# Linformer attention and a feed-forward layer on one core: k and v projections placed next to a burst of quarter-array matmuls, and v's last heads projected ahead of the third tile of values in the opening

## Chip, cores, metric

One core of one Trainium2 chip. The metric is the device time of one execution in microseconds.

## The reference, cut to what matters

```python
# q, k, v: (8 batches, 8 heads, 1024, 64); E, F: (64, 1024)
k_proj = np.einsum('ks,bhsd->bhkd', E, k)
v_proj = np.einsum('ks,bhsd->bhkd', F, v)
scores = q @ k_proj^T / sqrt(64)
attn   = exp(scores - max) / (sum(...) + 1e-9)
x      = (attn @ v_proj), heads side by side      # (8192, 512)
h      = x @ w_in                                  # (8192, 2048)
out    = (h * sigmoid(1.702 h)) @ w_out            # (8192, 512)
```

The last two lines are nearly all of the arithmetic. The kernel cuts the 8192 tokens into 16 blocks of 512; two blocks make a batch.

## The kernel before

The kernel writes its own order of instructions. Blocks are a first layer (16 groups of 4 full-array matmuls, slots 0 to 15) and a second (8 half-tiles of 8 full-array matmuls, slots `O` to `O + 7`). Attention work for later blocks is put between them by `at(block, slot, ...)`. TensorE's results land in PSUM; this kernel writes a bank of it anew only after another engine has read the results out, and it takes the banks of each pool in turn.

```python
def proj(b):                     # k and v of one batch: 128*64 tiles, two side by side
    def go():
        kvps[b] = f_tile([P, H, D])
        for j in range(J):
            for e, r in enumerate((LO, HI)):
                nc.tensor.matmul(kvps[b][r], eft[:, j, e * KP:(e + 1) * KP],
                                 (kt, vt)[e][b][:, :, j, :],
                                 start=(j == 0), stop=(j == J - 1))
    return go

def four(outs, lhsTs, rhss):     # 64*64 tiles, four at once: scores, denominators, numerators
    for i, ro in ((0, (LO, HI)), (1, (HI, LO))):
        for ri, r in zip((LO, HI), ro):
            nc.tensor.matmul(outs[i][r], lhsTs[i][ri], rhss[i][ri], start=True, stop=True)

# ... (cut) the opening
v_out(0, proj0(1, 0, 4), 0, 2)
for u in range(2):
    scores(0, u, 0)()
v_out(0, proj0(1, 4, 2), 2, 1)
for p in range(3):
    tok(0, p, 0)()
v_out(0, proj0(1, 6, 2), 3, 1, nc.scalar.copy)
for p in range(3):
    x_tr(0, p, 0)()
tok(0, 3, 0)()
q_tr(0, 1)()
x_tr(0, 3, 0)()

# ... (cut) where the projections and the bursts go
for b in range(2, B):
    j = max(2, NB2 * b - 3)
    at(j, 2, proj(b))
    at(j, 3, kv_out(b))          # DVE copies k and v out of the projection's PSUM bank
    if b > 2:
        at(NB2 * b - 4, O, q_dma(b))
for j in range(3, NBLK - 2):
    for u in range(2):
        if j + 3 < NBLK:
            at(j, O + 5 * u, scores(j + 3, u))
        at(j, O + 5 * u, norm(j + 2, u))
    if j + 3 < NBLK:
        at(j, O + 6, gelu_table)
```

The softmax here doesn't subtract the row's maximum and nothing guards it: scores larger than these inputs give would overflow.

Of the kernel before, what the change touches and what calls it, by code (L numbers as in the profile page):

```python
# [17 lines left out]
def kernel(ctx, tc, q, k, v, E, F,  # L18
                                                     moe_w_in, moe_w_out, out):
    nc = tc.nc  # L20
    B, H, S, D = q.shape
# [4 lines left out]
    NB2 = S // 512  # L26
# [90 lines left out]
    def f_tile(shape, dt=F32):  # L117
        return ps_f.tile(shape, dt, name="f_ps")
# [20 lines left out]
    def proj(b):  # L139
# [9 lines that stand above are left out]
    def proj0(e, h0, n):  # L149
        ps = f_tile([P, n, D])  # L150
        for j in range(J):
            nc.tensor.matmul(ps, eft[:, j, :], (kt, vt)[e][0][:, h0:h0 + n, j, :],
                             start=(j == 0), stop=(j == J - 1))
        return ps
# [14 lines left out]
    def v_out(b, v_ps, p0, n, cp=nc.vector.tensor_copy):  # L169
        if b < 2:  # L170
            if n == 1:
                for r, t in ((LO, p0 % 2), (HI, 1 - p0 % 2)):
                    cp(vxs[b][r, 2 * p0 + t, :D], v_ps[HI, t, :])
            else:
                vv = v_ps[HI].rearrange("k (u x) d -> k u x d", x=4)
                vx = vxs[b][:, 2 * p0:2 * (p0 + n), :D].rearrange("k (u x) d -> k u x d", x=4)
                for r, xs_ in ((LO, X_LO), (HI, X_HI)):
                    cp(vx[r, :, xs_], vv[:, :, xs_])
        if b > 0:
            vv = v_ps[HI].rearrange("k (u x) d -> k u x d", x=4)  # L180
            for r, xs_ in ((LO, X_LO), (HI, X_HI)):
                nc.vector.tensor_copy(vqs[b % 2][r].rearrange("k (u e) d -> k u e d", e=2), vv[:, :, xs_, :])

    def kv_out(b):
        def go():
            ps = kvps.pop(b)
            k_b = att.tile([KP, H, D], BF16, name="k_b")
            nc.vector.tensor_copy(k_b, ps[LO])
            if b > 1:
                nc.sync.dma_start_transpose(out=kts[b % 2], in_=k_b.rearrange("k h d -> k (h d)"))  # L190
            v_out(b, ps, 0, HP)
            kbs[b] = k_b
        return go

    def q_tr(b, g):
        def go():
            if g == 0:
                qT[b] = att.tile([P, J, HP, P], BF16, name="qT")
            t_ps = f_tile([P, 2, HP, P], BF16)
            for jj in range(2):  # L200
                j = 2 * g + jj
                if b == 0:
                    for h in range(H):
                        r = h % 2 * D
                        nc.tensor.transpose(t_ps[r:r + D, jj, h // 2, :], qt[0][:, h, j, :], ident)  # L205
                else:
                    for p in range(HP):
                        nc.tensor.transpose(  # L208
                            t_ps[:, jj, p, :],
                            qt[b][:, j, 2 * p:2 * p + 2, :].rearrange("s t d -> s (t d)"), ident)  # L210
            nc.vector.tensor_copy(qT[b][:, 2 * g:2 * g + 2], t_ps)  # L211
        return go

    def q_dma(b):
        def go():
            qT[b] = att.tile([P, J, HP, P], BF16, name="qT")
            nc.sync.dma_start_transpose(out=qT[b].rearrange("r j p s -> r (j p) s"),
                                        in_=qt[b].rearrange("s j h d -> s (j h d)"))
        return go

    def four(outs, lhsTs, rhss):
# [5 lines that stand above are left out]
    def scores(h, u, half=None):  # L227
        b, c = divmod(h, NB2)
        j0, n = (c * JB, JB) if half is None else (c * JB + half * JB // 2, JB // 2)
        ts = slice(j0 * P - c * TB, (j0 + n) * P - c * TB)  # L230

        def go():
            if h not in expT:
                expT[h] = att.tile([P, HP, TB], BF16, name="expT", bufs=3)
            s_ps = [f_tile([P, n * P]) for _ in range(2)]
            four(s_ps, [kts[b % 2][:, 2 * u + i, :] for i in range(2)],
                 [qT[b][:, j0:j0 + n, 2 * u + i, :] for i in range(2)])
            for i in range(2):
                nc.scalar.activation(expT[h][:, 2 * u + i, ts], s_ps[i], AF.Exp, scale=scale)  # L239
        return go  # L240
# [4 lines left out]
    def x_of(h):  # L245
        if h not in xT:
            xT[h] = att.tile([P, KC, TB], BF16, name="xT", bufs=3)
        return xT[h]

    def norm(h, u):  # L250
        def go():
            e = [expT[h][:, 2 * u + i, :] for i in range(2)]
            d_ps = [ps_d.tile([P, TB], F32, name="d_ps") for _ in range(2)]
            four(d_ps, [ones, ones], e)
            n_ps = [ps_n.tile([P, TB], F32, name="n_ps") for _ in range(2)]
            four(n_ps, [vqs[h // NB2 % 2][:, 2 * u + i, :] for i in range(2)], e)
            for i in range(2):
                rden = att.tile([P, TB], F32, name="rden")
                nc.vector.reciprocal(rden, d_ps[i])  # L259
                nc.vector.tensor_tensor(x_of(h)[:, 2 * u + i, :], n_ps[i], rden, op=ALU.mult)  # L260
        return go
# [5 lines left out]
    def tok(h, p, half):  # L267
        def go():
            d_ps = f_tile([P, 4, D + 1]) if (h, half) == (0, 0) and p > 1 else                 ps_d.tile([P, 4, D + 1], F32, name="d_ps")
            for i in range(2):  # L270
                t = 2 * half + i
                nc.tensor.matmul(d_ps[:, 2 * i:2 * i + 2, :].rearrange("s t d -> s (t d)"),  # L272
                                 expT[h][:, p, t * P:(t + 1) * P],
                                 vxs[h // NB2][:, 2 * p:2 * p + 2].rearrange("r t d -> r (t d)"),
                                 start=True, stop=True)
            rd = work.tile([P, 4, 1], F32, name="rd")
            nc.vector.reciprocal(rd, d_ps[:, :, D:])  # L277
            xs[h, p, half] = work.tile([P, 4, D], BF16, name="x_sb", bufs=4)
            nc.vector.tensor_tensor(xs[h, p, half], d_ps[:, :, :D], rd.to_broadcast([P, 4, D]), op=ALU.mult)
        return go  # L280

    def x_tr(h, p, half):
        def go():
            x_sb = xs.pop((h, p, half)).rearrange("s (i t) d -> s i (t d)", i=2)
            n_ps = ps_n.tile([P, 2, P], BF16, name="n_ps")
            for i in range(2):
                nc.tensor.transpose(n_ps[:, i, :], x_sb[:, i, :], ident)  # L287
            cp = nc.scalar.copy if (h, half) == (0, 0) else nc.vector.tensor_copy
            cp(x_of(h)[:, p, half * TB // 2:(half + 1) * TB // 2], n_ps.rearrange("r i s -> r (i s)"))
        return go  # L290
# [53 lines left out]
    def at(j, slot, *fs):  # L344
        fill.setdefault((j, slot), []).extend(fs)

    O = FC
# [6 lines left out]
    v_out(0, proj0(1, 0, 4), 0, 2)  # L354
    for u in range(2):
        scores(0, u, 0)()
    v_out(0, proj0(1, 4, 2), 2, 1)
    for p in range(3):
        tok(0, p, 0)()
    v_out(0, proj0(1, 6, 2), 3, 1, nc.scalar.copy)  # L360
    for p in range(3):
        x_tr(0, p, 0)()
    tok(0, 3, 0)()
    q_tr(0, 1)()
    x_tr(0, 3, 0)()

# [27 lines left out]
        at(1, O + 3 + p, x_tr(2, p, 0), x_tr(2, p, 1))  # L394
    at(2, 1, norm(3, 0))
    at(2, 11, norm(3, 1))
    for b in range(2, B):
        j = max(2, NB2 * b - 3)
        at(j, 2, proj(b))
        at(j, 3, kv_out(b))  # L400
        if b > 2:
            at(NB2 * b - 4, O, q_dma(b))
    for j in (1, 2):
        at(j, O + 5, gelu_table)
    at(2, O + 5, norm(4, 0))
    at(3, 4, norm(4, 1))
    for j in range(3, NBLK - 2):
        for u in range(2):
            if j + 3 < NBLK:
                at(j, O + 5 * u, scores(j + 3, u))  # L410
            at(j, O + 5 * u, norm(j + 2, u))
        if j + 3 < NBLK:
            at(j, O + 6, gelu_table)

    def filled(j, slot):
        for f in fill.pop((j, slot), []):
# [45 lines left out]
```

## Time and profile before

| | before |
|---|---|
| time, median of the first 3 runs | 518.31 us (518.21 to 518.4) |
| TensorE busy | 98% of the span, clock 1.0 |
| VectorE (DVE), ScalarE (ACT) busy | 49%, 51% |
| one steady batch (two blocks) | 60.71 us |

A timeline line gives the start and length in us, the engine, the source line, the output and input, the array tile of a matmul (128*128 full, 128*64 half, 64*64 quarter), the operand's shape and the count. A bracket says how long the engine had been idle and what released it. Ends of matmuls are modelled, so all arithmetic uses starts. The lines for before stand in the prediction.

### The profile page before, as it was taken

Reading aid. Unit: us, or ns where it says so; the run is one execution under the profiler, and the core shown is the slowest. Engines: PE = TensorE matmul, PEld = TensorE weight load, DVE = VectorE, ACT = ScalarE, POOL = GpSimd, SP = SyncE. Lnnn points to the kernel's source line nnn. Section 1 sums busy time; section 2 is a strip of 40 time slices with the busy share of each in tenths; the row PEclk is TensorE's granted clock in tenths of the full one; section 3 lists DMA queues with packets and bytes.
Section 4 is the critical chain, followed back from the end, with each engine's and each line's share of the span. In section 5 each row is a group of like instructions: output and inputs, shape, how many; then the busy total and the mean of one; then the engine's idle time right before and its main releaser. Section 6 shows DMA issues by size and latency. Waiting matters only on the chain.

```text
span 516.5 us, 6729 instructions
## 1 busy us (share of the span) xinstructions
PE 506.9 (98%) x2856; PEld 233.2 (45%) x2856; DVE 251.4 (49%) x231; ACT 264.0 (51%) x439; POOL 77.4 (15%) x96
## 2 busy tenths in 40 slices
PE   6899999999999999999999999999999999999997
PEld 3584454444444444444444444444444444444444
DVE  3533324766774672818547282655818275560000
ACT  1575464555646456474555645465473646344351
POOL 6442620821510024000510000000000000000000
PEclk9999999999999999999999999999999999999999
DMA  9999999999996039550694201060200101010102
GB/s 162 197 203 207 217 180 182 165 191 159 241 152 162 1 90 166 106 133 0 147 176 121 53 41 48 0 164 0 84 4 1 81 1 81 1 82 1 81 1 82
DMA packets 113950, 53.78 MB, mean 104 GB/s; under 512 B 87680, under 2 KB 111488, under 8 KB 112000
## 3 DMA queue, kind: packets, MB, share of 16 engines
q0 software_dynamic: 84384, 29.37, 50.2%
q1 hardware_dynamic: 29456, 23.73, 16.6%
q8 instruction: 22, 0.36, 0.3%
q10 hardware_dynamic: 80, 0.26, 0.1%
q14 instruction: 8, 0.07, 0.0%
HBM read 59.24 MB, written 16.78 MB: 147 GB/s over the span
## 4 chain that ended last, share of the span: by engine, by line
PE 94%; DMA 4%; POOL 1%; issue 0%; DVE 0%; DVEq 0%; POOLq 0%
PE f_ps L333 43%; PE f_ps L301 42%; PE f_ps L144 3%; DMA w_in_sb<-in_moe_w_in_dram 2%; DMA v_sb<-in_v_dram 2%; PE f_ps L225 2%; PE d_ps L225 1%; PE n_ps L225 1%; PE f_ps L325 1%; PE n_ps L287 0%; PE d_ps L272 0%; PE f_ps L208 0%; POOL k_sb L57 0%; PE f_ps L205 0%; POOL q_sb L57 0%
## 5 line engine op out<-in xcount | busy, mean ns | idle before, releaser
L259 DVE RECIPROCAL rden<-d_ps 128x512 f32<-128x512 f32 x52 | 174.4, 3353 | 149.0 <-PE d_ps L225 149.0
L301 PE MATMUL f_ps<-xT,w_in_sb 128*128 128x512 bf16 (+1 forms) x1088 | 228.4, 367 | 0.2
L333 PE MATMUL f_ps<-w_out_sb,gT 128*128 128x512 bf16 x1008 | 227.0, 379 | 0.0
L304 ACT ACTIVATE gT<-f_ps 128x512 bf16<-128x512 f32 (+1 forms) x268 | 153.7, 575 | 85.4 <-PE f_ps L301 84.4
L301 PEld LDWEIGHTS <-w_in_sb 128*128 128x128 bf16 x1088 | 104.5, 98 | 116.4 <-issue 4.3
L333 PEld LDWEIGHTS <-gT 128*128 128x128 bf16 x1008 | 95.7, 98 | 120.4 <-issue 11.1
L336 ACT COPY o_sb<-f_ps 128x512 f32<-128x512 f32 x63 | 37.0, 587 | 133.5 <-PE f_ps L333 123.7
L63 POOL DMA_DIRECT2D q_sb<-in_q_dram x56 | 49.1, 894 | 67.5 <-DMA k_sb<-in_k_dram 27.7
L239 ACT ACTIVATE expT<-f_ps 128x512 bf16<-128x512 f32 (+1 forms) x68 | 35.2, 574 | 14.4 <-PE f_ps L225 14.4
L260 DVE TENSOR_TENSOR xT<-n_ps,rden 128x512 bf16<-128x512 f32 x52 | 36.0, 692 | 5.4
L327 DVE COPY o_sb<-f_ps 128x256 f32<-128x256 f32 x1 | 0.4, 424 | 50.9 <-PE f_ps L325 50.9
L57 POOL DMA_DIRECT2D k_sb<-in_k_dram x9 | 7.8, 864 | 103.7 <-PE f_ps L144 101.4
L239 ACT ACT_TABLE_LOAD x13 | 16.7, 1283 | 4.7 <-PE f_ps L225 4.5
L243 ACT ACT_TABLE_LOAD x14 | 18.0, 1283 | 0.3
L225 PE MATMUL f_ps<-qT,kt 64*64 64x512 bf16 (+1 forms) x136 | 13.8, 386 | 0.4 <-ACT expT L239 0.4
L144 PE MATMUL f_ps<-k_sb,eft 128*64 128x512 bf16 x56 | 13.4, 382 | 0.0
L144 PE MATMUL f_ps<-v_sb,eft 128*64 128x512 bf16 x56 | 13.4, 382 | 0.0
L211 DVE COPY qT<-f_ps 128x1024 bf16<-128x1024 bf16 x8 | 5.5, 692 | 12.4 <-PE f_ps L205 6.8
L277 DVE RECIPROCAL rd<-d_ps 128x4 f32<-128x4 f32 x22 | 3.8, 175 | 15.5 <-PE d_ps L272 15.4
L225 PEld LDWEIGHTS <-kt 64*64 64x64 bf16 x136 | 4.0, 103 | 14.3 <-issue 14.3
L225 PE MATMUL d_ps<-expT,ones 64*64 64x512 bf16 x104 | 10.2, 381 | 0.0
L225 PE MATMUL n_ps<-expT,vq 64*64 64x512 bf16 x104 | 10.0, 376 | 0.0
(57 smaller groups left out, 127.0 us busy)
## 6 DMA issues: line engine op xcount, KB each, us to landing
out_dram<-o_sb SPq DMA_DIRECT2D x15, 1024.0 KB, 4.5
k_sb<-in_k_dram POOLq DMA_DIRECT2D x7, 1024.0 KB, 13.5
v_sb<-in_v_dram POOLq DMA_DIRECT2D x7, 1024.0 KB, 10.7
q_sb<-in_q_dram POOLq DMA_DIRECT2D x56, 128.0 KB, 11.1
w_in_sb<-in_moe_w_in_dram POOLq DMA_DIRECT2D x8, 256.0 KB, 12.7
w_out_sb<-in_moe_w_out_dram POOLq DMA_DIRECT2D x4, 512.0 KB, 14.7
k_sb<-in_k_dram POOLq DMA_DIRECT2D x2, 512.0 KB, 8.0
out_dram<-o_sb SPq DMA_DIRECT2D x3, 256.0 KB, 2.0
```

The costliest lines, as they stand in the source:

```text
L57: nc.gpsimd.dma_start(out=dst[b][:, h:h + n, js:js + jn], in_=sv[:, h:h + n, js:js + jn])
L63: nc.gpsimd.dma_start(out=qt[b][:, j], in_=qv[:, j])
L144: nc.tensor.matmul(kvps[b][r], eft[:, j, e * KP:(e + 1) * KP], (kt, vt)[e][b][:, :, j, :], start=(j == 0), stop=(j == J - 1))
L225: nc.tensor.matmul(outs[i][r], lhsTs[i][ri], rhss[i][ri], start=True, stop=True)
L239: nc.scalar.activation(expT[h][:, 2 * u + i, ts], s_ps[i], AF.Exp, scale=scale)
L243: nc.scalar.preload_act_table(AF.Gelu_apprx_sigmoid)
L259: nc.vector.reciprocal(rden, d_ps[i])
L260: nc.vector.tensor_tensor(x_of(h)[:, 2 * u + i, :], n_ps[i], rden, op=ALU.mult)
L301: nc.tensor.matmul(h_ps, w_in_sb[:, kc, fc * P:(fc + 1) * P], xT[j][:, kc, ts], start=(kc == 0), stop=(kc == KC - 1))
L304: nc.scalar.activation(gts[j][:, fc, ts], h_ps, AF.Gelu_apprx_sigmoid)
L333: nc.tensor.matmul(o_ps[n], gts[j][:, fc, n * P:(n + 1) * P], w_out_sb[:, fc, :], start=(fc == 0), stop=(fc == FC - 1))
L336: nc.scalar.copy(osb[j][:, n, :], o_ps.pop(n))
```

## The change

TensorE pays something each time the shape of its tiles changes (0.09 to 0.12 us in the trace of before, worked out in the prediction). The change puts the projections of batches 4 to 7 directly ahead of a burst of quarter tiles, so that one return to full tiles falls away. In the opening it is meant to fill waits for DVE with other work.

```diff
     for u in range(2):
         scores(0, u, 0)()
+    for p in range(2):
+        tok(0, p, 0)()
     v_out(0, proj0(1, 4, 2), 2, 1)
-    for p in range(3):
-        tok(0, p, 0)()
+    x_tr(0, 0, 0)()
     v_out(0, proj0(1, 6, 2), 3, 1, nc.scalar.copy)
-    for p in range(3):
-        x_tr(0, p, 0)()
+    tok(0, 2, 0)()
+    x_tr(0, 1, 0)()
     tok(0, 3, 0)()
+    x_tr(0, 2, 0)()
     q_tr(0, 1)()
     x_tr(0, 3, 0)()
 ...
-    for b in range(2, B):
-        j = max(2, NB2 * b - 3)
-        at(j, 2, proj(b))
-        at(j, 3, kv_out(b))
-        if b > 2:
-            at(NB2 * b - 4, O, q_dma(b))
 ...
+    at(2, 2, proj(2))
+    at(2, 3, kv_out(2))
+    for b in range(3, B):
+        j = NB2 * b - 4
+        at(j, O, q_dma(b))
+        at(j, O + 6, proj(b), kv_out(b))
 ...
             if j + 3 < NBLK:
-                at(j, O + 5 * u, scores(j + 3, u))
-            at(j, O + 5 * u, norm(j + 2, u))
+                at(j, O + 6 * u, scores(j + 3, u))
+            at(j, O + 6 * u, norm(j + 2, u))
         if j + 3 < NBLK:
-            at(j, O + 6, gelu_table)
+            at(j, O + 7, gelu_table)
```

## The prediction

> **What bounds the kernel now.** I read the page's busy line and chain first, then TensorE's timeline over one pair of steady blocks, then its weight loads, then the opening.
>
> ```profile
> PE 506.9 (98%) x2856; PEld 233.2 (45%) x2856; DVE 251.4 (49%) x231; ACT 264.0 (51%) x439; POOL 77.4 (15%) x96
> ...
> PEclk9999999999999999999999999999999999999999
> ...
> PE 94%; DMA 4%; POOL 1%; issue 0%; DVE 0%; DVEq 0%; POOLq 0%
> ```
>
> TensorE is busy 98% of the span at full clock and carries 94% of the chain; every other engine is about half idle. So only two things can move the time: what TensorE itself spends between its matmuls, and the few places where it waits. The timeline of blocks 3 and 4 (two blocks make one batch) shows the first kind (start, duration, engine, line):
>
> ```profile
> 170.07 1.89 PE L333 MATMUL f_ps<-w_out_sb,gT 128*128 128x512 bf16 x8
> 171.89 0.41 PE L225 MATMUL f_ps<-qT,kt 64*64 64x512 bf16 x4
> 172.13 0.39 PE L225 MATMUL d_ps<-expT,ones 64*64 64x512 bf16 x4
> 172.34 0.39 PE L225 MATMUL n_ps<-expT,vq 64*64 64x512 bf16 x4
> 172.66 8.81 PE L333 MATMUL f_ps<-w_out_sb,gT 128*128 128x512 bf16 x40
> ...
> 185.64 2.75 PE L301 MATMUL f_ps<-xT,w_in_sb 128*128 128x512 bf16 x12
> 188.32 0.40 PE L144 MATMUL f_ps<-k_sb,eft 128*64 128x512 bf16 x1
> ...
> 190.17 11.40 PE L301 MATMUL f_ps<-xT,w_in_sb 128*128 128x512 bf16 x52
> 201.40 1.89 PE L333 MATMUL f_ps<-w_out_sb,gT 128*128 128x512 bf16 x8
> ```
>
> Work with starts only, since the ends are modelled. The 64 matmuls of an undisturbed first layer (156.25 to 170.07) take 13.82 us, 0.216 us each. A burst of 12 quarter tiles (64*64, four at once) should cost 3 x 0.216 = 0.65 us, but the gap from 171.89 to 172.66 is 0.77, and the burst began 0.09 late (170.07 + 8 x 0.216 = 171.80). So it costs about 0.09 to enter and 0.12 to leave. Scores, denominators and numerators inside it follow each other with 0.24, 0.21: no further toll between bursts of one shape. The k and v projection (128*64, two at once) should take 8 x 0.216 = 1.73: it starts 0.09 after 185.64 + 12 x 0.216 = 188.23, and from 188.32 to 190.17 is 1.85, again 0.12 to leave. **One detour costs 0.21 to 0.22 us**, in either shape. The same sum for whole layers agrees: 201.40 - 185.64 = 15.76, less 13.82, less 1.73, is 0.21.
>
> The weight loads show why:
>
> ```profile
> 185.42 2.47 PEld L301 LDWEIGHTS <-w_in_sb 128*128 128x128 bf16 x12
> 188.32 1.44 PEld L144 LDWEIGHTS <-eft 128*64 128x64 bf16 x16 [0.42 <-issue]
> 190.16 1.84 PEld L301 LDWEIGHTS <-w_in_sb 128*128 128x128 bf16 x10 [0.41 <-issue]
> ```
>
> Between equal shapes a load starts 0.22 us ahead of its matmul (185.42 against 185.64) and is hidden; where the shape changes it starts with the matmul (188.32, 190.16), after some 0.4 us without a load. A load takes 98 to 109 ns by the groups, about the size of the toll.
>
> **What the Trainium skill says.** "TensorE: Matmul & The Clock Gate", section "Back-to-back issue gap", gives N / 2.4 + 2.5 ns warm, so 215.8 ns at N = 512; the trace's 0.216 agrees. Its section "The mechanism" says that a weight load overlaps running matmuls only where the row group differs; the quarter tiles and the half-column tiles share rows with what runs before them, and the trace's loads at a change of shape are indeed exposed, though loads between equal full-array matmuls are hidden here. "TensorEngine Tiling (Array Packing)", section "Key Properties", says: "Changing tiling mode (not just tile) drains the TensorE". The trace agrees for full to quarter, full to half and back, with 0.09 to 0.12 us a step. By that sentence half (128*64) to quarter (64*64) is a change of mode too; no place in this trace puts the two side by side.
>
> **The change, part one: projections beside a burst.** Nothing is added or removed: the same instructions stand in another order. From the order of the built program:
> - Batch 2's projection stays where it was: 0.
> - Batch 3's moves from early in block 3 to block 2 behind the seventh half-tile of the second layer, but block 2's last quarter burst stands one half-tile before. It is still alone between full matmuls: 0.
> - Batches 4 to 7 go to the seventh half-tile of blocks 4, 6, 8, 10, and that block's second burst moves there from the sixth. The order is projection, scores, denominators, numerators, with no full matmul between: four merges.
>
> Before, such a pair makes four changes of shape: 0.09 + 0.12 + 0.09 + 0.12 = 0.42 to 0.43. After, it makes three: in 0.09, half to quarter x, out 0.12. The unknown is x. Since a change of mode exposes a weight load of about the same length (0.10), I take x = 0.10. Saving: 0.12 + 0.09 - 0.10 = 0.11 to 0.12 per merge, **0.46 us for four**. If x were nothing it would be 4 x 0.21 = 0.86; if x cost as much as leaving and entering, 0.
>
> Does the new place make a new wait? I looked at each:
> - Data: v of batch 4 is issued at 120.17 us and lands some 11 us later, its projection is needed at 183; batch 3's v is issued at 98.40 and needed near 122. Room enough.
> - DVE: the reciprocals of the burst before end at 180.8 (two of 3.4 us and two of 0.7 from 172.55), before the projection ends near 184.9. k_b and vq (0.68 + 0.87) are done near 186.5, earlier than today (191.9).
> - PSUM: by the built program's banks the first layer takes, after the burst, the two score banks, then the projection's, then the second layer's. The third is wanted about 1.7 us after the second layer ends (187.7 before the saving), and DVE has freed it at 186.5.
> - ACT: the last output copy is now ahead of the Gelu table load, which costs 1.28 us:
>
> ```profile
> 183.10 1.28 ACT L243 ACT_TABLE_LOAD   x1
> 185.84 0.59 ACT L336 COPY o_sb<-f_ps 128x512 f32<-128x512 f32 x1 [1.46 <-PE f_ps L333]
> 186.76 0.60 ACT L304 ACTIVATE gT<-f_ps 128x512 bf16<-128x512 f32 x1 [0.34 <-PE f_ps L301]
> ```
>
>   Today it hides in ACT's idle time. After, in these times, copy to 186.4, table to 187.7, first Gelu to 188.3 in place of 187.4. Its bank is wanted by the fifth group, at 185.64 + 4 x 0.864 = 189.1. So the first Gelu is later by 0.9 us, and 0.8 us of margin are left. At one activation per 0.5 to 0.6 us against one group per 0.86 us, ACT catches up. This happens in ten blocks; cost 0.
>
> **Part two: the opening.** Today TensorE waits there for DVE: 0.42 us for v's heads 4 and 5, then 0.26, 0.26 and 0.17 for tiles of values. After, the first two tiles come ahead of those heads. Stepping through with the trace's durations (reciprocal 0.18, multiply 0.42, two copies 0.47, release to matmul about 0.06), the first full matmul moves from 21.15 to about 20.9: 0.2 to 0.3 us earlier. But the chain shows what comes next:
>
> ```profile
> 15.19 11.37 DMA w_in_sb<-in_moe_w_in_dram
> 26.56 0.05 issue
> 26.61 0.61 PE f_ps L301 x4
> ```
>
> and the weight loads show three waits for pieces of w_in:
>
> ```profile
> 24.12 0.77 PEld L301 LDWEIGHTS <-w_in_sb 128*128 128x128 bf16 x8 [0.16 <-DMA w_in_sb<-in_moe_w_in_dram]
> ...
> 25.26 0.33 PEld L301 LDWEIGHTS <-w_in_sb 128*128 128x128 bf16 x4 [0.15 <-DMA w_in_sb<-in_moe_w_in_dram]
> ...
> 26.60 0.33 PEld L301 LDWEIGHTS <-w_in_sb 128*128 128x128 bf16 x4 [0.24 <-DMA w_in_sb<-in_moe_w_in_dram]
> ```
>
> That piece is issued at 15.19, behind other loads and not behind TensorE, so it lands at 26.56 however early TensorE comes. The gain is waited away there: 0. An opening made slower by a few tenths would be hidden too.
>
> **Sum:** 518.31 - 0.46 - 0 = 517.85 us.
>
> **Rivals.** (1) *Half to quarter is free*: the two need only halves or quarters reloaded. For: bursts of one shape follow freely. Against: the skill's sentence and overlapping rows. It makes 517.45. (2) *No saving*: the middle change costs a full detour. Against: no single change in the trace exceeds 0.13. It makes 518.3. (3) *ACT becomes a wait*: table load behind the copy, or a bank freed late. If it stalled ten blocks by 0.3 us: plus 3 us, 520.9; the margin above speaks against it. (4) *The opening counts*: if the pieces of w_in came earlier than the profile shows, up to 0.3 us more, 517.6.
>
> **Range and chances.** The three values of x span 517.45 to 518.3; repeated runs of the kernel before differ by 0.2. I choose 517.3 to 518.4. Two per cent is 10.4 us; all tolls concerned add up to less than 2 us, so faster is next to excluded; slower needs a stall of 1 us in every block.
>
> **What would show it.** In blocks 4, 6, 8, 10 the step from the projection's last matmul to the scores' first is 0.22 plus x: 0.31 to 0.32 by me, 0.22 by rival 1. From one batch to the next (185.64 to 246.35, 60.71) the period falls by 0.11 to 0.12. Block 2 keeps its toll. The first w_in matmul starts near 20.9, yet the wait on w_in near 26.6 grows by as much and ends at the same time. First-layer matmuls in the opening of a block show no wait on ACT. I am wrong if TensorE waits on ACT or a PSUM bank after the burst, if the time falls over 1 us, or if the opening's gain survives past 30 us.

## More of the kernel before

All executions compared here fall into two groups, told apart by the mean granted TensorE clock listed for each: 0.998 or more ("full clock"), and 0.997 or less ("late clock").

Where tenths of a microsecond matter, full-clock executions are compared with each other, and the traces decide.

## The result, and the profile after

The changed kernel took 517.69 us (median of 6, 517.26 to 518.8), the kernel before 518.47 us (median of 6, 518.21 to 519.78). The ratio is 0.9982, with a 95% interval of 0.9967 to 0.9996. A ratio here is the mean time of one kernel's fast runs over that of the other's of the same rounds, so it is not quite the ratio of the medians. 517.69 lies inside the predicted 517.3 to 518.4.

The profiled execution of the changed kernel happened to be a late-clock one (518.8 us, clock 0.997). Its page, to be read against that of before:

```profile
PE 507.8 (98%) x2856; PEld 234.3 (45%) x2856; DVE 251.0 (49%) x231; ACT 262.6 (51%) x439; POOL 77.3 (15%) x96
...
PEclk8999999999999999999999999999999999999999
...
PE 97%; DMA 1%; DVE 1%; ACT 1%; issue 0%; DVEq 0%; ACTq 0%
```

The engines are as busy as before. The first digit of the clock is 8 instead of 9, which belongs to a slower start of this one execution, as shown below. The chain no longer runs through the DMA of w_in, because w_in had landed in time here, as it had in e2 with the old opening. Neither is the change's doing.

TensorE in block 4, from the seventh half-tile of the second layer to the next first layer:

```profile
184.08 0.40 PE L144 MATMUL f_ps<-k_sb,eft 128*64 128x512 bf16 x1
...
185.62 0.38 PE L144 MATMUL f_ps<-k_sb,eft 128*64 128x512 bf16 x1
...
185.93 0.41 PE L225 MATMUL f_ps<-qT,kt 64*64 64x512 bf16 x4
...
186.70 1.90 PE L333 MATMUL f_ps<-w_out_sb,gT 128*128 128x512 bf16 x8
188.44 13.98 PE L301 MATMUL f_ps<-xT,w_in_sb 128*128 128x512 bf16 x64
202.25 1.89 PE L333 MATMUL f_ps<-w_out_sb,gT 128*128 128x512 bf16 x8
...
249.05 13.98 PE L301 MATMUL f_ps<-xT,w_in_sb 128*128 128x512 bf16 x64
```

Denominators and numerators (cut) follow the scores with 0.24 and 0.21 us, as before. The step from the last pair of the projection to the scores is 185.93 - 185.62 = 0.31 us, the same in all four blocks, of which the pair itself takes 0.216. **The change from half to quarter tiles costs 0.095 us**, as the prediction assumed (0.10). The next first layer takes 202.25 - 188.44 = 13.81 us, so nothing waits in it. The following batch's first layer starts at 249.05, so a batch takes 60.61 us, 0.10 less than before.

The weight loads of the same stretch:

```profile
184.08 1.44 PEld L144 LDWEIGHTS <-eft 128*64 128x64 bf16 x16 [0.42 <-issue]
185.93 0.11 PEld L225 LDWEIGHTS <-kt 64*64 64x64 bf16 x4 [0.41 <-issue]
...
186.70 1.41 PEld L333 LDWEIGHTS <-gT 128*128 128x128 bf16 x8 [0.41 <-issue]
```

The load for the scores starts with its matmul, at 185.93, as at the other two changes of shape: it is not hidden by the half tiles before it. Whether the step of 0.095 us is this load itself or something else that a change of shape brings, no run here separates.

ACT, whose table load now comes after the last output copy:

```profile
188.64 0.59 ACT L336 COPY o_sb<-f_ps 128x512 f32<-128x512 f32 x1 [1.18 <-PE f_ps L333]
189.24 1.28 ACT L243 ACT_TABLE_LOAD   x1
190.54 2.15 ACT L304 ACTIVATE gT<-f_ps 128x512 bf16<-128x512 f32 x4
```

The first Gelu starts 2.1 us after the first layer does (before: 1.1), and four of them follow without a pause. The first is through at 191.13 (at 0.60 us each), and the fifth group, which by the prediction's order of banks needs its bank, starts at 188.44 + 4 x 0.864 = 191.90: the margin of 0.8 us that the prediction gave. From the fifth Gelu on ACT waits for TensorE again.

**Why the profile's span is longer though the kernel is faster.** The table of stretches shows TensorE's busy time and granted clock (the last columns are clock, DMA share and GB/s) for 8 to 12 us. Before:

```profile
8.00:12.00 4.00, 3.49 (x25) 2.00 (x23) 1.33 (x3) 0.00 (x0) 1.60 (x3) 1.00 1.43 191
```

After, in this execution:

```profile
8.00:12.00 4.00, 3.61 (x17) 1.74 (x15) 1.05 (x2) 0.00 (x0) 0.86 (x2) 0.57 1.45 198
```

The clock was 0.57 of full there, so only 17 matmuls started instead of 25. The first v projection came at 16.41 instead of 14.95 us. The code up to that point is the same in both kernels, and both have the same TensorE idle stretch of 1.84 us just before (waiting for the cast of E and F). The Trainium skill, "TensorE: Matmul & The Clock Gate", section "What's actually happening", says that the clock is released and withdrawn by a free-running window of 3.4 us; that the same code falls on either side from one execution to the next agrees with it. The packed trace of this execution keeps the granted clock over time: full from 4.85 us, half from 8.27 to 11.68, then full to the end. That stretch is 3.41 us long, and so is the half clock in e6 (147.39 to 150.80), so the runs show the page's length. In the kernel before the clock was released at 4.21 us and not withdrawn, although its idle stretch, too, lay within the 3.41 us that followed; what decides it stays open.

This matters for reading the ratio. On the chip of the first four experiments, 6 of 11 executions of the kernel before were late-clock (mean 519.36 us against 518.06 in the other five), but only one of six in each kernel beside it. A ratio over all of them therefore flatters every kernel that was compared there.

### The profile page after: what moved, and what is told of

It reads as the page before. It is cut to its first block, busy times and chain, and to the rows that moved or that the text cites. A ratio compares the mean times of both kernels' runs of the same rounds, so it can differ in the third digit from the quotient of the medians.

```text
span 517.0 us, 6732 instructions
## 1 busy us (share of the span) xinstructions
PE 507.8 (98%) x2856; PEld 234.3 (45%) x2856; DVE 251.0 (49%) x231; ACT 262.6 (51%) x439; POOL 77.3 (15%) x96
## 4 chain that ended last, share of the span: by engine, by line
PE 97%; DMA 1%; DVE 1%; ACT 1%; issue 0%; DVEq 0%; ACTq 0%
PE f_ps L301 43%; PE f_ps L333 43%; PE f_ps L144 3%; PE f_ps L225 2%; PE d_ps L225 1%; PE n_ps L225 1%; DMA ef_f<-in_E_dram 1%; PE f_ps L123 1%; PE f_ps L325 1%; PE f_ps L152 1%; PE n_ps L287 1%; PE d_ps L272 1%; PE f_ps L205 0%; PE f_ps L208 0%; DVE x_sb L279 0%; ACT L127 0%
## 5 line engine op out<-in xcount | busy, mean ns | idle before, releaser
L304 ACT ACTIVATE gT<-f_ps 128x512 bf16<-128x512 f32 (+1 forms) x268 | 151.3, 575 | 64.7 <-PE f_ps L301 63.7
L188 DVE CAST k_b<-f_ps 64x512 bf16<-64x512 f32 x7 | 4.8, 679 | 24.9 <-PE f_ps L144 24.9
```

What stands on the lines that cost most here:

```text
L304: nc.scalar.activation(gts[j][:, fc, ts], h_ps, AF.Gelu_apprx_sigmoid)
```

## The experiments

"Full clock" below gives the number and mean of those executions. The three groups of four ran on one chip each. The kernel before had 518.06 (5 of 11), 518.06 (9 of 11) and 518.04 us (8 of 9) in them; the rest was late-clock, at 519.36, 519.39 and 519.47. By the verdicts of 2% all runs are "same" as the kernel before, except e6, which is "unclear" (1.0193 to 1.0232); the intervals of the others are 0.0012 to 0.0015 wide to either side. So the traces, not the ratios, carry the argument.

| run | full clock | all: ratio to before |
|---|---|---|
| e1_opening_only | 5 of 6: 518.12 | 0.9993 |
| e2_proj_only | 5 of 6: 517.54 | 0.9982 |
| e3_moved_not_adjacent | 5 of 6: 518.28 | 0.9995 |
| e4_two_more_merges | 5 of 6: 518.71 | 1.0002 |
| e5_merges_with_room | 4 of 6: 517.62 | 0.9994 |
| e6_four_pieces | 0 of 5 (all: 529.32) | 1.0213 |
| e7_old_opening_no_w_in_wait | 5 of 5: 517.50 | 0.9985 |
| e8_new_opening_no_w_in_wait | 4 of 6: 517.50 | 0.9992 |
| e9_changed_again | 5 of 5: 517.85 | 0.9990 |
| e10_projection_behind | 5 of 5: 518.45 | 1.0005 |
| e11_changed_longer_warm_up | 5 of 5: 517.61 | 0.9988 |
| e12_merges_and_warm_up | 5 of 5: 517.36 | 0.9983 |

Since openings vary by up to a microsecond from one execution to the next, I also cut each trace at one instruction that all kernels have, the transposes of q in the first block (line 205, between 32.79 and 33.82 us in the full-clock profiles), and compare what follows: "rest" is the time from that start to the start of DVE's last copy of the output (line 327, near 512 us).

### Which half of the change counts

e1: the first hunk of the diff alone. e2: the others alone.

> Only the opening's hunk of the change, the projections as before. Theory A (mine: the opening's gain is waited away at the third to fifth piece of w_in; the saving comes from four merges): the same as the kernel before within 0.15 us, first full matmul of w_in 0.2 to 0.3 us earlier relative to the first v projection, and the wait on w_in longer by as much. Rival B (the measured 0.9 us is twice my 0.46 because the opening counts too): 0.3 to 0.5 us faster than the kernel before.

> Only the projections' hunk, the opening as before. Theory A: all of the change's gain, 0.4 to 0.5 us faster than the kernel before by the steady part, with a step of 0.31 us from the projection's last pair to the scores and a batch period of 60.60 to 60.61 us. Rival B: about half of what the whole change gave, the rest missing.

e1's full-clock executions are 0.06 us above the kernel before, e2's 0.52 below. The rest after the cut is 479.72 us in e1 and in the kernel before (33.29 to 513.01), and 479.29 in e2 and in the changed kernel (34.25 to 513.54). So the projections are worth **0.43 us**, and they are the gain that the traces show; rival B falls.

TensorE in e2, with the old opening (first v projection, first matmul of w_in, the cut):

```profile
15.01 1.05 PE L152 MATMUL f_ps<-v_sb,eft 128*128 128x256 bf16 x8 [0.29 <-DMA v_sb<-in_v_dram]
...
21.20 0.89 PE L301 MATMUL f_ps<-xT,w_in_sb 128*128 128x256 bf16 x4
...
33.01 0.64 PE L205 MATMUL f_ps<-ident,q_sb 128*64 128x128 bf16 x16
```

And in e1, with the new one:

```profile
15.14 1.04 PE L152 MATMUL f_ps<-v_sb,eft 128*128 128x256 bf16 x8
...
21.17 0.89 PE L301 MATMUL f_ps<-xT,w_in_sb 128*128 128x256 bf16 x4
...
32.97 0.64 PE L205 MATMUL f_ps<-ident,q_sb 128*64 128x128 bf16 x16
```

From the first v projection to w_in is 6.19 us in the old opening, 6.03 in the new: 0.16 us gained. The waits for DVE on that way moved more than they shrank: 0.42, 0.27, 0.26 and 0.17 us in e2, 0.18, 0.39 and 0.51 in e1. In these two executions no wait for w_in shows, and the way from there to the cut is 11.81 and 11.80: the 0.16 us is kept. In the profile of before the same way took 12.14, with three waits for w_in.

### Is it the neighbourhood or the new place?

```diff
-                at(j, O + 6 * u, scores(j + 3, u))
-            at(j, O + 6 * u, norm(j + 2, u))
+                at(j, O + 5 * u, scores(j + 3, u))
+            at(j, O + 5 * u, norm(j + 2, u))
-            at(j, O + 7, gelu_table)
+            at(j, O + 6, gelu_table)
```

> The whole change, but the second burst of each block goes back to the sixth half-tile, so that eight full matmuls stand between it and the projection. Theory A (adjacency saves): batch period back at 60.71 us, time 0.45 us above the changed kernel. Rival C (the new place of the projection saves, by an easier DVE and ACT schedule): period stays at 60.61, time as the changed kernel's.

The projection stays in its new place, but eight full matmuls stand between the burst and it. Its first layers one batch apart:

```profile
188.17 13.98 PE L301 MATMUL f_ps<-xT,w_in_sb 128*128 128x512 bf16 x64
...
248.89 13.98 PE L301 MATMUL f_ps<-xT,w_in_sb 128*128 128x512 bf16 x64
```

A batch takes 60.72 us, as before (60.71), where e2 has 60.61 (187.20 to 247.81). The time is 518.28 us at full clock, 0.7 above e2 and no better than before; the rest after the cut is 479.81, 0.09 above the old value (block 2 is longer by that much). So adjacency saves, not the place. Its opening is the new one with waits for w_in (weight loads):

```profile
24.45 0.77 PEld L301 LDWEIGHTS <-w_in_sb 128*128 128x128 bf16 x8 [0.28 <-DMA w_in_sb<-in_moe_w_in_dram]
...
25.76 0.33 PEld L301 LDWEIGHTS <-w_in_sb 128*128 128x128 bf16 x4 [0.33 <-DMA w_in_sb<-in_moe_w_in_dram]
...
27.09 0.33 PEld L301 LDWEIGHTS <-w_in_sb 128*128 128x128 bf16 x4 [0.24 <-DMA w_in_sb<-in_moe_w_in_dram]
```

From the first v projection to the cut it took 18.47 us, as before (18.34): here the opening's gain is waited away, as predicted. From the third of these loads to the cut is 6.69 us in e3 (27.09 to 33.78), in e4 (26.44 to 33.13) and in e12 (26.13 to 32.82), all with the new opening, and also in the profile of before with the old one (26.60 to 33.29): where TensorE has to wait for that piece, its landing sets the time and the opening does not. Both cases exist.

### Two more merges, a miss, and its repair

e4 moves batch 2's and batch 3's projections beside a burst as well; e5 also moves one burst of denominators back by three groups (the edit is shortened here).

```diff
-    at(2, 1, norm(3, 0))
-    at(2, 11, norm(3, 1))
+    at(2, 14, norm(3, 1))
-    at(2, 2, proj(2))
-    at(2, 3, kv_out(2))
+    at(2, 2, proj(2), kv_out(2), norm(3, 0))
+    at(2, O + 5, proj(3), kv_out(3))      # ahead of scores(5, 1)
-    at(3, 4, norm(4, 1))
+    at(3, 7, norm(4, 1))                  # e5 only
```

> The changed kernel with batch 2's and batch 3's projections put beside a burst too. Theory A: two more merges of 0.116 us each, 0.23 us below the changed kernel. If DVE is late for the denominators in block 2 (burst at the fifteenth group of the first layer) there is a wait on TensorE there and the time rises by that wait instead.

> The two further merges again, but batch 4's last denominators three groups later in block 3, so that DVE is done with the ones before. The first try lost 1.15 us there on a bank still held for DVE. Theory A: the wait is gone, two merges of 0.116 us remain: 0.23 us below the changed kernel, about 0.75 us below the kernel before, among executions with the clock above 0.998.

e4 was slower, 518.71 us. The wait was there, though not in block 2 where I had feared it but in block 3:

```profile
130.25 0.40 PE L225 MATMUL d_ps<-expT,ones 64*64 64x512 bf16 x2
130.82 0.40 PE L225 MATMUL d_ps<-expT,ones 64*64 64x512 bf16 x2 [0.17 <-DVE rden L259]
...
131.62 0.40 PE L225 MATMUL n_ps<-expT,vq 64*64 64x512 bf16 x2 [0.38 <-DVE xT L260]
```

DVE now copies k and v (1.6 us) ahead of two reciprocals of 3.4 us, so the denominators' banks come free later than their next user wants them. The first 20 matmuls of block 3's first layer and this burst last 131.95 - 125.84 = 6.11 us against 4.96 in the changed kernel: 1.15 us lost for 0.23 to be gained. e5 removes the wait: no TensorE wait is left after the opening, and the rest is 479.09 us, 0.20 below the kernels with four merges. Blocks 2 and 3 take 64.91 us (91.13 to 156.04) in place of 65.12 (92.09 to 157.21 in the changed kernel), 0.21 less: two merges at the 0.10 that each of the others gives, a little under the 0.23 expected. In times, 517.62 us, the gain over e2 does not show.

### Paying the toll more often

```diff
+            for i, slot in enumerate((2, 3, 5, 6)):
+                at(j, slot, proj(b, range(2 * i, 2 * i + 2)))
+            at(j, 7, kv_out(b))
```

> The kernel before with the projections of batches 3 to 7 cut into four pieces, each between full matmuls: fifteen detours more. Theory A (each detour costs 0.21 to 0.22 us whatever is in it): 15 x 0.216 = 3.2 us slower than the kernel before, period of a batch up by 0.65 us. If the cost were a matter of the instructions' number or of the banks and not of the change of shape, nothing near it: the number of matmuls is the same.

The kernel before, with five projections cut in four. Read from the trace, a batch takes 61.40 us (192.36 to 253.76), 0.69 more than before: 0.23 per additional detour, of which 0.02 is the slower first pair of each piece. That supports the toll. The total, 11 us more, is no measure of it, because this edit brought a wait of its own in block 3: DVE came to the copy of batch 3's k only at 138.42 us, behind two reciprocals of the denominators placed among the pieces, so its transposed form landed late, and during the stall the clock fell to half (from 147.39 us on; four quarter matmuls take 0.64 instead of 0.41 us):

```profile
147.82 0.64 PE L226 MATMUL f_ps<-qT,kt 64*64 64x512 bf16 x4 [4.70 <-DMA kt<-k_b]
```

I had not foreseen this; the expectation of 3.2 us for the total failed.

### The opening without the wait for w_in

Both kernels have the changed projections, and read the first two pieces of w_in over and over in the first half-block. Their outputs are wrong, which doesn't matter for the times. e7 has the old opening, e8 the new.

```diff
+        wc = fc % 4 if j == 0 and ts.start == 0 else fc
-            nc.tensor.matmul(h_ps, w_in_sb[:, kc, fc * P:(fc + 1) * P], xT[j][:, kc, ts],
+            nc.tensor.matmul(h_ps, w_in_sb[:, kc, wc * P:(wc + 1) * P], xT[j][:, kc, ts],
```

> The changed kernel with the opening of before, and the first half of the first block reads only the first two pieces of w_in again and again (the result is wrong on purpose), so that nothing waits for later pieces. Partner of the next run: their difference is the opening's worth without that wait. Against the kernel with the same opening and the pieces read in full, at most 0.5 us faster.

> The same with the new opening (wrong on purpose too). Theory A (the new opening's first full matmul comes 0.16 us earlier, and the wait for w_in eats it): 0.1 to 0.2 us faster than its partner, among executions with the clock above 0.998. Rival D (something else behind the opening, DVE's and ACT's queues, eats it): no difference from its partner, with a wait on DVE or ACT near 26 us in both.

In the traces: 6.19 us from the first v projection to w_in in e7, 6.04 in e8, then 11.80 and 11.81 to the cut. Nothing behind the opening eats the gain when w_in is there, so rival D falls. The times do not settle it: both means are 517.50, with one e8 execution at 518.17 and the other three at 517.21 to 517.33; e7 is at 517.34 to 517.60.

### The changed kernel again, the order turned round, and a longer warm-up

```diff
# e10: for batches 4 to 7, registered after scores and norm
+    for b in range(4, B):
+        at(NB2 * b - 4, O + 6, proj(b), kv_out(b))
# e11: the changed kernel; e12: e5
-    warm(12)
+    warm(16)
```

> The changed kernel itself once more, beside the next three on one chip, and beside the kernel before on the chip that the experiments used. By the traces so far: merges worth 0.44 us, opening worth 0 to 0.16; 0.45 to 0.6 us below the kernel before among executions with the clock above 0.998, and about 1.3 us more in those below.

> The changed kernel with the four projections behind the burst instead of ahead of it (quarter to half in place of half to quarter, and their copies on DVE behind the reciprocals). Theory A (a change of shape costs about 0.1 us in any direction): the step from the last quarter tile to the projection is 0.31 us too. The projection's bank is then held until DVE is through, so three banks are left for the first layer; by the built order its fourth group waits for the first Gelu, which stands behind the table load: 0.1 to 0.3 us of wait on ACT in each of four blocks, 0.4 to 1.2 us above the changed kernel.

> The changed kernel with 16 instead of 12 matmuls of warm-up, to shorten TensorE's idle stretch before the first transposes from 1.8 to about 1 us. Theory E (the executions that are 1.3 us longer are those in which the clock falls again in that stretch): none or fewer with a clock below 0.998, the others unchanged. If the stretch has nothing to do with it: the same mix, or up to 0.9 us longer where the warm-up delays the transposes.

> The best of the parts: six merges, the new opening and the longer warm-up. 0.23 us below the run with the longer warm-up alone; about 0.7 us below the kernel before among executions with the clock above 0.998.

**e9**, the changed kernel once more: 517.85 us at full clock, 0.19 below before, less than expected; one execution at 518.37 pulls it up. The rest after the cut is 479.29 us, as in the first trace. With the five of the first comparison, ten full-clock executions average 517.73, about 0.3 below the kernel before on the later chips. The repeat thus shows the gain clearly in the trace and only roughly in the time.

**e10**, quarter to half. The step is 0.31 us in this direction too:

```profile
183.24 0.39 PE L225 MATMUL n_ps<-expT,vq 64*64 64x512 bf16 x4
183.55 0.40 PE L144 MATMUL f_ps<-k_sb,eft 128*64 128x512 bf16 x1
...
187.14 14.13 PE L301 MATMUL f_ps<-xT,w_in_sb 128*128 128x512 bf16 x63
201.11 1.89 PE L333 MATMUL f_ps<-w_out_sb,gT 128*128 128x512 bf16 x8
```

But the next first layer takes 201.11 - 187.14 = 13.97 us instead of 13.81, and 13.96 to 13.97 in the other three such blocks (the count of 63 is a missing record); the weight loads pause for 0.27 us ahead of the fourth group, at 189.89. The first Gelu, behind the table load, starts at 189.24 and ends at 189.83, so this is the wait on ACT that was expected, 0.15 to 0.16 us in each of four blocks. The rest is 479.90 us, 0.61 more than in e9, and the time 518.45, 0.6 more. That the fourth group and not the fifth meets the first Gelu fits the bank that the projection still holds: DVE copies k only at 191.57, behind its reciprocals. The change's order, projection first, avoids it.

**e11 and e12**: none of the ten executions was late-clock, but on this chip the kernel before had only one in nine and e9 none in five, so theory E is neither shown nor refuted (in e11's trace the idle stretch is gone). e12 is the fastest kernel here: 517.36 us, 0.68 below the kernel before (0.13%), 0.25 below e11 with the same warm-up; its rest of 479.08 us is 0.21 below e11's 479.29, like e5's 479.09.

## Why the prediction was right or wrong

- **The range**: 517.3 to 518.4 holds the kernel before as well (518.31), so that the time lies in it proves little. The mechanism is shown by the traces and by e2, e3 and e6.
- **The toll of a detour, 0.21 to 0.22 us**: right. Moving the projection without making it a neighbour keeps it (e3), and cutting it in pieces multiplies it (e6, 0.23 each).
- **The unknown x = 0.10 for half to quarter**: right, 0.095, and the same in the other direction (e10). Rivals 1 and 2, x of nothing and of a full detour, fall.
- **Four merges, 0.46 us**: right, 0.43 by the rest after the cut and 0.52 by e2's full-clock times; a batch is 0.10 us shorter, not 0.11 to 0.12. Batches 2 and 3 gained nothing, as the built order said (65.12 us for blocks 2 and 3 in both kernels); e5's trace recovers it, 0.21 for two merges.
- **No new wait on ACT, DVE or a bank**: right, first layers stay at 13.81 us. e4 and e10 show how near it is: the same projections in other places, or behind the burst, do make such a wait. One reading was off without harm: v of batch 4 takes 17.4 us from issue to landing, not 11, long before it is needed.
- **The opening is 0.2 to 0.3 us faster**: mis-sized, 0.16; new waits for DVE came in place of the old ones (the longest 0.51 us, for a tile of values).
- **"The gain is waited away there: 0"**: right only for executions in which w_in is late, like the one profiled before. I took one profile's landing at 26.56 us for the rule. In e1, e2 and e5 no such wait shows, and then the 0.16 us stays. By the prediction's own sign ("if the opening's gain survives past 30 us") this part was wrong for such executions; it is its rival 4, at half the size given there. Over all executions of e1 the effect is not measurable (0.06 us above before).
- **"The wait on w_in near 26.6 grows by as much"**: not seen in the changed kernel's profile, because that execution was late for another reason. e4 shows it: 0.15, 0.31 and 0.23 us in place of 0.16, 0.15 and 0.24, so 0.14 more in sum. In e3 (0.28, 0.33 and 0.24) it is 0.30 more, since its piece also landed 0.13 us later after the first v projection.
- **4 x 0.21 = 0.86 for rival 1**: a slip, it is 0.84 (0.86 is 4 x 0.215); nothing rests on it.
- **The base of the sum**: I subtracted from 518.31 and did not know of the late-clock executions. The ratio of 0.9982 is 0.9 us, twice what the traces show. The late-clock share of the kernel before accounts for such an excess on the chip of e1 to e4. In the first comparison it does so only in part: without the two longest executions of before (519.34 and 519.78 us; their clocks are not on record) and the late one of the changed kernel the means are 518.37 and 517.61, still 0.75 us apart, while e9 beside its own kernel before was 0.19 below. Where the remaining 0.3 us come from stays open. Why the kernel before had more late-clock executions on one chip stays open.

## What to carry to other kernels

On a saturated TensorE each excursion from full to partial tiles costs about 0.2 us here, half on the way in and half on the way out, and putting two kinds of partial tiles next to each other saves one of the four steps of a pair, not all. Before moving such a piece, look at who frees its PSUM bank and what stands in front of that on DVE or ACT: a merge worth 0.1 us made a wait of 1 us where that was overlooked. For gains this small, compare executions of the same clock and cut the traces at a common instruction, because an opening that varies by a microsecond hides them.

## What the Trainium skill lacked or had wrong

- "TensorEngine Tiling (Array Packing)", section "Key Properties", says that a change of mode drains the engine but gives no size. Here: full to quarter or half 0.09 to 0.10 us, back to full 0.10 to 0.12 (with a slightly longer step behind it), half to quarter and quarter to half 0.095.
- "TensorE: Matmul & The Clock Gate", section "The mechanism", says in one sentence that weight loads overlap running matmuls only where the row group differs, and in another that a load into the background weight buffer is pulled ahead as well; the prediction took the first alone. Between full-array matmuls of the same rows they start 0.22 us ahead of their own matmul here and are hidden, so the second is the one that fits. Neither says that a load starts only with its matmul where the tile's shape changes, as at 185.93 us here.
- The same page warns in its section "Why this matters for your kernels" of idle gaps above about 3 us. Here an idle stretch of 1.84 us before the first transposes was followed, in one execution, by a clock of 0.57 from 8 to 12 us, and in another by none; executions with the lower clock were 0.9 to 1.4 us longer. That this idle stretch is the cause is not shown: the edit that removes it (e11) met no late-clock executions, but hardly any stood beside it either.
